# Loading a spectral filter in 18 loads of 2 pieces, each on half the partitions, in place of 28 loads of 3 pieces over all partitions

## Chip, cores and metric

The kernel runs on one core of a Trainium2 chip. The metric is the device time of one execution in microseconds (us), as the median of several runs. The spans and moments that profiles give are counted from the first instruction and come out about 1.8 us shorter than that time.

## The reference, cut to what matters

```python
x = A_x                                              # 1 x 2048 x 512, bfloat16
X = rfft2(layernorm(x)) * (w_r + 1j * w_i)           # the filter: 2048 x 257, real and imaginary part
h = x + irfft2(X)
h2 = h + MLP_over_the_rows(layernorm(layernorm(h)))  # two large products with B_w1, B_w2
```

Row 64q + r of the filter (q = 0 to 31) meets a spectrum row kept at free position r; row 64q + (64 − r) is its mirror. The kernel keeps 32 positions, and on each of the 128 partitions a fixed combination of q, of the half (itself or its mirror, `ss`), and of real or imaginary part (`reim`).

## The kernel before

The constants L and H of the transforms say which partition holds which combination:

```python
for jj, ss, sgn, j in kinds:
    ...
    for k2 in range(NS2):
        pre = 8 * k2 + 4 * jj + 2 * ss        # the partition; the imaginary part is at pre + 1
```

Neighbours in q are thus four partitions apart. The filter is loaded in three pieces of rows; each load fills 32 partitions, four apart, with runs of 512 bytes:

```python
pieces = [(0, 8), (8, 18), (18, 32)]
for pi, (ta, tb) in enumerate(pieces):
    for comp, wsrc in enumerate((A_w_r, A_w_i)):
        wv = wsrc.rearrange("(q r) k -> q r k", r=64)
        for reim in range(2):
            parts = [(0, ta, tb, wv[:, ta:tb, 1:257])]
            lo = ta
            if ta == 0:
                parts.append((1, 0, 1, wv[:, 32:33, 1:257]))
                lo = 1
            parts.append((1, lo, tb, wv[:, 64 - lo:64 - tb:-1, 1:257]))
            for ss, a, b, src in parts:
                dma(..., "sp", W[2 * ss + reim:NP:4, a:b, comp, :], src, ..., group=f"W{pi}", wgroup=f"W{pi}")
```

The loads of one piece share one semaphore, so a reader waits for the whole piece. The readers are 16 multiplications on VectorE, called P0 to P15 below:

```python
def emit_P(c):          # reads filter rows 2c and 2c + 1
    return eng.tensor_tensor(P[:, :, :, :], x.unsqueeze(2).broadcast_to(...), W[:, 2 * c:2 * c + 2, :, :], ALU.mult)
# VectorE's fixed order: ... P0 P1 ... P3 P2 ... P4 ... P5 ... P7 P6 ... P9 P8 ... P10 P11 ... P13 P12 ... P14 P15
```

PE turns each P into 8 short products (I0 to I15, in a fixed order too). Beside the filter, GpSimd's queue loads the biases of the MLP, that of the first product in single elements of 2 bytes, that of the second in runs of 32 bytes:

```python
gate = [o for o in K.ops if o.name == "Ye15"]        # a ScalarE copy near 16 us
dma("ld_b1a", "pool", B1s[:, 0:10], B_b1[0:1280].rearrange("(t p) -> p t", p=NP), 2560, ..., after=gate)
```

## Time and profile before

| | before |
|---|---|
| time, median | 130.94 us in the first 3 runs, 130.69 in the 6 around the comparison |
| span of the profiled run | 129.0 us |
| filter loads: number, last issued, last landed | 28, 25.95 us, 30.1 us |
| VectorE's wait for the filter | 1.75 us, at P9 |
| last product of the filter stage on PE | 37.68 us |
| granted clock | 1.0 |

In the profile, PE is the matmul engine, PEld its weight loads, DVE VectorE, ACT ScalarE, POOL GpSimd and SP or SPq the sync engine and its queue. A timeline row gives start, duration, what was done, how often, and in brackets the idle time just before with what ended it. A windows row gives a stretch and its length; the busy time of PE, PEld, DVE, ACT and POOL; then the granted clock, the share of the 16 DMA engines, and GB/s. The lines themselves are shown in the prediction.

### The profile page before, as it was taken

Reading aid. Unit: us, or ns where it says so; the run is one execution under the profiler, and the core shown is the slowest. Engines: PE = TensorE matmul, PEld = TensorE weight load, DVE = VectorE, ACT = ScalarE, POOL = GpSimd, SP = SyncE. Lnnn points to the kernel's source line nnn. Section 1 sums busy time; section 2 is a strip of 40 time slices with the busy share of each in tenths; the row PEclk is TensorE's granted clock in tenths of the full one; section 3 lists DMA queues with packets and bytes.
Section 4 is the critical chain, followed back from the end, with each engine's and each line's share of the span. In section 5 each row is a group of like instructions: output and inputs, shape, how many; then the busy total and the mean of one; then the engine's idle time right before and its main releaser. Section 6 shows DMA issues by size and latency. Waiting matters only on the chain.

```text
span 129.0 us, 2045 instructions
## 1 busy us (share of the span) xinstructions
PE 122.8 (95%) x786; PEld 74.6 (58%) x786; DVE 65.0 (50%) x141; ACT 65.0 (50%) x137; POOL 12.5 (10%) x33
## 2 busy tenths in 40 slices
PE   6998979999899999999999999999999999999990
PEld 2356657778576655555544444456666666666660
DVE  1689949986978999968650000000422423323322
ACT  4789879999868999897777712222000000000000
POOL 0068970220000000000000000000000000000000
PEclk9999999999999999999999999999999999999999
DMA  3999888899999999999100000000112111121121
GB/s 91 357 393 366 253 208 179 231 340 387 407 425 425 417 418 409 239 401 394 41 0 0 0 0 0 5 0 0 41 50 72 41 67 60 41 81 41 41 84 41
DMA packets 16505, 22.71 MB, mean 176 GB/s; under 512 B 1552, under 2 KB 12304, under 8 KB 16368
## 3 DMA queue, kind: packets, MB, share of 16 engines
q1 hardware_dynamic: 15808, 21.66, 48.2%
q10 hardware_dynamic: 576, 0.92, 2.1%
q0 software_dynamic: 112, 0.01, 0.4%
q8 instruction: 6, 0.10, 0.3%
q14 instruction: 3, 0.02, 0.1%
HBM read 20.49 MB, written 2.10 MB: 175 GB/s over the span
## 4 chain that ended last, share of the span: by engine, by line
PE 71%; SPq 18%; DVE 3%; DMA 3%; issue 2%; DVEq 0%
PE ps L844 29%; PE ps L962 28%; SPq L490 18%; PE ps L771 5%; DMA W<-in_A_w_i_dram 3%; PE ps L692 3%; PE ps L808 2%; DVE P L674 2%; PE ps L968 2%; PE ps L911 1%; DVE TT L709 1%; DVE OUT L974 1%; PE ps L864 0%; PE ps L533 0%; PE ps L801 0%
## 5 line engine op out<-in xcount | busy, mean ns | idle before, releaser
L844 PE MATMUL ps<-HH,W 128*128 128x512 bf16 (+1 forms) x170 | 39.6, 379 | 0.0
L962 PE MATMUL ps<-GT,W 128*128 128x512 bf16 (+1 forms) x165 | 35.9, 379 | 0.0
L974 DVE SCALAR_TENSOR_TENSOR OUT<-ps,B2f,H 128x512 bf16<-128x512 f32 x16 | 12.0, 752 | 46.7 <-PE ps L962 24.4
L962 PEld LDWEIGHTS ps<-GT,W 128*128 128x128 bf16 (+1 forms) x165 | 23.8, 144 | 11.9
L844 PEld LDWEIGHTS ps<-HH,W 128*128 128x128 bf16 (+1 forms) x170 | 16.9, 100 | 17.5 <-issue 0.2
L944 ACT ACTIVATE GT<-ps,B1f 128x512 bf16<-128x512 f32 (+1 forms) x11 | 7.0, 692 | 12.7 <-PE ps L844 12.7
L818 DVE TENSOR_TENSOR H<-ps,X 128x512 bf16<-128x512 f32 x14 | 9.7, 691 | 4.0 <-PE ps L808 3.4
L824 ACT ACTIVATE SQ<-H,nm 128x512 bf16<-128x512 bf16 x14 | 10.1, 720 | 2.7 <-DVE H L818 2.4
L674 DVE TENSOR_TENSOR P<-Xsb,W 128x1024 bf16<-128x1024 bf16 x16 | 10.4, 684 | 1.9 <-DMA W<-in_A_w_i_dram 1.8
L559 DVE BATCH_NORM_STATS2 st<-X 128x6 f32<-128x512 bf16 x13 | 8.3, 679 | 3.2 <-DMA X<-in_A_x_dram 3.2
L692 PE MATMUL ps<-Hm,P 128*128 128x128 bf16 x128 | 9.1, 220 | 0.7 <-DVE TT L709 0.6
L781 ACT ACTIVATE EO<-ps 128x512 bf16<-128x512 f32 x15 | 8.8, 586 | 0.9 <-PE ps L771 0.7
L637 PE MATMUL ps<-E,Y 128*128 128x256 bf16 x64 | 8.5, 273 | 0.7 <-ACT Y L607 0.7
L771 PE MATMUL ps<-GD,TT 128*128 128x256 bf16 x60 | 9.0, 273 | 0.0
L692 PEld LDWEIGHTS ps<-Hm,P 128*128 128x128 bf16 x128 | 7.4, 98 | 2.7 <-issue 1.1
L533 PE MATMUL ps<-WM 128*128 128x512 bf16 (+1 forms) x20 | 7.6, 540 | 1.2 <-DVE eps L525 1.2
L593 PE MATMUL ps<-FS,X 128*128 128x256 bf16 x64 | 7.8, 273 | 0.5 <-POOL FS L577 0.5
L665 ACT ACTIVATE Xsb<-ps 128x1024 bf16<-128x1024 f32 (+1 forms) x9 | 8.0, 886 | 0.7 <-PE ps L652 0.4
L577 POOL TENSOR_SCALAR FS<-F,rs 128x256 bf16<-128x256 bf16 x16 | 7.4, 481 | 7.5 <-DMA F<-c_F 6.9
L641 ACT ACTIVATE Bsb<-ps 128x512 bf16<-128x512 f32 x13 | 7.3, 594 | 1.2 <-PE ps L637 1.2
L771 PEld LDWEIGHTS ps<-GD,TT 128*128 128x128 bf16 x60 | 5.8, 98 | 3.0 <-ACT EO L781 0.2
L593 PEld LDWEIGHTS ps<-FS,X 128*128 128x128 bf16 x64 | 5.4, 97 | 3.0 <-POOL FS L577 1.5
(70 smaller groups left out, 98.3 us busy)
## 6 DMA issues: line engine op xcount, KB each, us to landing
W<-in_B_w_dram SPq DMA_DIRECT2D x8, 688.0 KB, 11.0
W<-in_B_w_dram SPq DMA_DIRECT2D x10, 512.0 KB, 17.7
out_dram<-OUT SPq DMA_DIRECT2D x16, 128.0 KB, 1.7
X<-in_A_x_dram SPq DMA_DIRECT2D x4, 256.0 KB, 6.2
F<-c_F SPq DMA_DIRECT2D x4, 256.0 KB, 6.6
IF<-c_IF SPq DMA_DIRECT2D x1, 1024.0 KB, 6.5
W<-in_A_w_r_dram SPq DMA_DIRECT2D x4, 224.0 KB, 4.2
W<-in_A_w_i_dram SPq DMA_DIRECT2D x4, 224.0 KB, 4.2
```

The lines of the kernel that those rows point to most:

```text
L490: return eng.dma_start(dst, src)
L593: r = eng.matmul(ps[:, b, 256 * u:256 * u + 256].rearrange("p (a b) -> p a b", a=2), X[:, n2, 128 * t:128 * t + 128], fr if t < 2 else fa, ...
L637: r = eng.matmul(o, Y[:, k, c, :], E[:, k, :].rearrange("p (h r) -> p h r", h=2), start=(i == 0), stop=(i == 3), skip_group_check=True)
L674: return eng.tensor_tensor(P[:, :, :, :], x.unsqueeze(2).broadcast_to([NP, 2, 2, 256]), W[:, 2 * c:2 * c + 2, :, :], ALU.mult)
L692: r = eng.matmul(o, P[:, h, m, par::2], Hm[:, v, m, :].rearrange("p (m r) -> p m r", r=4), start=(h == 0 and m == 0 and (par == 0 or b != ...
L771: r = eng.matmul(o, TT[:, q, n2, par, :], GD[:, par, q, :], start=(i == 0), stop=(i == 3), skip_group_check=True)
L781: return eng.activation(eo[:, :], ps[:, bE, :], ACT.Copy)
L818: K.op(f"h{n2}", "dve", lambda e, eng: eng.tensor_tensor(H[:, n2, :], ps[:, bA, :], X[:, n2, :], ALU.add), ins=[ps[:, bA, :], X[:, n2, :]] ...
L824: K.op(f"sq{n2}", "act", lambda e, eng: eng.activation(sq[:, :], hsrc, ACT.Square, bias=nm[:, n2, 0:1], accum_out=s2t[:, n2, 0:1]), ins=[h ...
L844: return eng.matmul(ps[0:Mt, bank, :], W1[:, n2, 128 * t:128 * t + Mt], HH[:, n2, :], start=(n2 == 0), stop=(n2 == 15), skip_group_check=True)
L962: r = eng.matmul(ps[:, b, :], W2[t][0:Kt, n2::16], GT[0:Kt, t, :], start=(t == 0), stop=(t == NFT - 1), skip_group_check=True)
L974: K.op(f"fin{n2}", "dve", lambda e, eng, n2=n2, b=b: eng.scalar_tensor_tensor(OUT[:, n2, :], ps[:, b, :], B2f[:, n2:n2 + 1], H[:, n2, :], ...
```

## The change

Its intent is fewer issues on the sync engine: the mirrored half moves to partitions 64 to 127. The odd mirrored row 32 is then one load for both `reim`, and the pieces become two.

```diff
-                pre = 8 * k2 + 4 * jj + 2 * ss
+                pre = 64 * ss + 4 * k2 + 2 * jj
 (the same once more, for H)
-    pieces = [(0, 8), (8, 18), (18, 32)]
+    pieces = [(0, 12), (12, 32)]
     for pi, (ta, tb) in enumerate(pieces):
         for comp, wsrc in enumerate((A_w_r, A_w_i)):
             wv = wsrc.rearrange("(q r) k -> q r k", r=64)
 (the loads of before, shown above, go)
+            lo = max(ta, 1)
+            for ss, src in ((0, wv[:, ta:tb, 1:257]), (1, wv[:, 64 - lo:64 - tb:-1, 1:257])):
+                a = lo if ss else ta
+                for reim in range(2):
+                    dma(f"ld_w{comp}_{pi}_{ss}_{reim}", "sp", W[64 * ss + reim:64 * ss + 64:2, a:tb, comp, :], src, ...)
+            if pi == 0:
+                dma(f"ld_w{comp}_{pi}_m", "sp", W[64:128, 0, comp, :], wv[:, 32, 1:257].unsqueeze(1).broadcast_to([32, 2, 256]), ...)
```

More of the change, by code (lines that the diff above doesn't have):

```diff
@@ L98, in build_consts @@
             for k2 in range(NS2):
-                pre = 8 * k2 + 4 * jj + 2 * ss
+                pre = 64 * ss + 4 * k2 + 2 * jj
                 if special:
@@ L513, in build_kernel @@
             wv = wsrc.rearrange("(q r) k -> q r k", r=64)
-            for reim in range(2):
-                parts = [(0, ta, tb, wv[:, ta:tb, 1:257])]
-                lo = ta
-                if ta == 0:
-                    parts.append((1, 0, 1, wv[:, 32:33, 1:257]))
-                    lo = 1
-                parts.append((1, lo, tb, wv[:, 64 - lo:64 - tb:-1, 1:257]))
-                for ss, a, b, src in parts:
-                    dma(f"ld_w{comp}_{pi}_{reim}_{ss}_{a}", "sp", W[2 * ss + reim:NP:4, a:b, comp, :], src, 32 * 512 * (b - a),
+            lo = max(ta, 1)
+            for ss, src in ((0, wv[:, ta:tb, 1:257]), (1, wv[:, 64 - lo:64 - tb:-1, 1:257])):
+                a = lo if ss else ta
+                for reim in range(2):
+                    dma(f"ld_w{comp}_{pi}_{ss}_{reim}", "sp", W[64 * ss + reim:64 * ss + 64:2, a:tb, comp, :], src, 32 * 512 * (tb - a),
                         prio=1.0 + pi, group=f"W{pi}", wgroup=f"W{pi}")
+            if pi == 0:
+                dma(f"ld_w{comp}_{pi}_m", "sp", W[64:128, 0, comp, :], wv[:, 32, 1:257].unsqueeze(1).broadcast_to([32, 2, 256]), 64 * 512,
+                    prio=1.0 + pi, group=f"W{pi}", wgroup=f"W{pi}")
     K.op("mk_eps", "dve", lambda e, eng: eng.memset(eps[:, 0:1], LN_EPS), outs=[eps[:, 0:1]], occ=70.0, lat=130.0, prio=0)
```

## The prediction

> **What bounds the kernel now.** I started with the page's busy shares: PE 122.8 of 129.0 us. The granted clock is 1.0 throughout. The kernel is one long row of PE work, so a change counts only where PE is held back by something else. The chain that ended last says where that is:
>
> ```profile
> PE 71%; SPq 18%; DVE 3%; DMA 3%; issue 2%; DVEq 0%
> ```
>
> From about 30 us on the chain is PE. Before that it is the issue of DMAs by the sync engine (SPq), closed by one transfer. The chain in order of time shows the joint:
>
> ```profile
> 25.29 0.63 SPq L490
> 25.95 4.18 DMA W<-in_A_w_i_dram
> 30.23 1.29 DVE P L674 x2
> 31.52 0.60 DVE TT L709
> ```
>
> So the last filter load is issued at 25.95, lands 4.18 us later, and two filter multiplications (P, L674) start at that instant. The list of waits gives the price, in us in total, times, longest:
>
> ```profile
> DVE P L674 <- DMA W<-in_A_w_i_dram: 1.8, 1, 1.8
> ```
>
> Only one multiplication waits for the filter. VectorE's timeline shows which, and what is behind it (start, duration):
>
> ```profile
> 19.86 1.29 DVE L674 TENSOR_TENSOR P<-Xsb,W 128x1024 bf16<-128x1024 bf16 x2
> ...
> 26.42 1.28 DVE L674 TENSOR_TENSOR P<-Xsb,W 128x1024 bf16<-128x1024 bf16 x2
> 27.78 0.69 DVE L709 CAST TT<-ps 128x512 bf16<-128x512 f32 x1
> 30.23 1.29 DVE L674 TENSOR_TENSOR P<-Xsb,W 128x1024 bf16<-128x1024 bf16 x2 [1.75 <-DMA W<-in_A_w_i_dram]
> 31.44 0.68 DVE L709 CAST TT<-ps 128x512 bf16<-128x512 f32 x1
> 32.04 1.28 DVE L674 TENSOR_TENSOR P<-Xsb,W 128x1024 bf16<-128x1024 bf16 x2
> ```
>
> P number c reads filter rows 2c and 2c+1, and VectorE's fixed order is P0 P1 P3 P2 P4 P5 P7 P6 P9 P8 and so on. The pair at 26.42 is P7, P6; the pair at 30.23 is P9, P8, and P9 is the first to need the third piece (rows 18 to 31). From 30.23 VectorE has no gap until 36.9, and PE idles 0.63 us for it. The stage therefore follows VectorE, and the end of the kernel follows the stage.
>
> The loads' issue, from the sync engine's timeline:
>
> ```profile
> 6.76 4.00 SPq L490 DMA_DIRECT2D W<-in_A_w_r_dram  x6
> 10.80 3.87 SPq L490 DMA_DIRECT2D W<-in_A_w_i_dram  x6
> 14.71 2.59 SPq L490 DMA_DIRECT2D W<-in_A_w_r_dram  x4
> 17.35 3.69 SPq L490 DMA_DIRECT2D W<-in_A_w_i_dram  x4
> 21.08 2.64 SPq L490 DMA_DIRECT2D W<-in_A_w_r_dram  x4
> 23.76 2.82 SPq L490 DMA_DIRECT2D W<-in_A_w_i_dram  x4
> ```
>
> 28 issues take 19.8 us, some 0.66 each (one of 1.70), whether 16 KB or 224 KB. Is it the issue or the transfer that limits? The windows (last two columns: share of the 16 DMA engines, GB/s) say: mostly the issue.
>
> ```profile
> 14.00:16.00 2.00, 2.00 (x19) 1.32 (x16) 1.78 (x3) 1.60 (x4) 1.84 (x6) 1.00 0.77 209
> 16.00:18.00 2.00, 1.31 (x13) 1.09 (x12) 0.57 (x1) 1.30 (x4) 1.76 (x6) 1.00 0.83 205
> 26.00:28.00 2.00, 2.00 (x26) 1.49 (x25) 1.92 (x4) 2.00 (x4) 0.78 (x2) 1.00 1.14 341
> ```
>
> While 128 to 160 KB pieces are issued, only 205 to 209 GB/s move; once 224 KB pieces come, the same kind of packet reaches 341. By the trace's transfer records the filter is 8192 packets of 512 B (4.19 MB), nearly all of 27 ns, up to 674 of them in a microsecond. They start at 12.3 us, behind x and the constants.
>
> **What the Trainium skill says.** (1) "SBUF — State Buffer", section "Door 1: The DMA port swizzle": 64 neighbouring partitions (0 to 63, or 64 to 127) reach only 8 of SBUF's 16 DMA ports; it measured 196 GB/s for partitions 0 to 63 against 328 for all, with 218 as the asymptote. Every filter load of before steps through the partitions by 4 over all 128, so over all 16 ports, and 341 GB/s agrees. No load of before lies in one half, so its trace can't confirm the 196. (2) The same page, "Can I just issue two DMAs to hit both halves?": two DMAs, one per half, gained 6% together, "they serialize". (3) "DMA: Bandwidth & Descriptors", "Queues, rings and completion order": a DMA is split over up to 16 engines and each takes its ring in order, so loads of one half queue ahead of loads of the other. The lines above show no contrary case. (4) Same page, "Rules for kernel authors": coalesce small transfers. The 16 KB issues, as dear as 224 KB ones, agree.
>
> **The change, part by part.**
> Removed: 10 issues, 10 × 0.66 = 6.6 us of the sync engine. 18 issues end at 6.76 + 18 × 0.66 = 18.6, instead of 26.6. From 12.3 us on about 8 loads are already queued, so the transfers, not the issues, set the pace: 300 GB/s of issue in the first piece (196 KB per 0.66 us), 500 in the second.
> Kept: 8192 packets, all instructions of the compute engines and their shapes (L and H only have rows permuted).
> Moved: first, the pieces are rows 0 to 11 (3072 packets) and 12 to 31 (5120). P7 and P6, at 26.42, now need the last load of all; before, they needed the second of three pieces. Second, each load lies in one half of the partitions, on 8 ports.
> What the ports make of it, an estimate: a port that passes 27.2 GB/s (the skill's figure) takes 512 / 27.2 = 18.8 ns per packet, and two engines share it, so 37.6 ns instead of 27 for each engine. 8 ports give 425 packets per us, 218 GB/s; the skill's own measurement, 196, gives 383. I take 405 (207 GB/s).
> First piece: 12.3 + 3072 / 405 = 19.9, plus about 0.6 until the last packet counts: 20.5, where P0 now starts at 19.86. A short wait.
> Second piece: 12.3 + 8192 / 405 + 0.6 = 33.1. P7 wants it at 26.42, so VectorE waits 6.7 us. Behind P7 the stage needs what it needs now without the 1.75 us wait: 37.68 (end of the stage's matmuls) − 26.42 − 1.75 = 9.5 us, all VectorE's. Little is made up in the wait, because PE's next products need P6. The stage ends at 33.1 + 9.5 = 42.6 instead of 37.7: +4.9.
> After the stage: the identity, GD, IF (1.3 MB) and W1 are issued earlier but are carried after the filter. At 420 GB/s the first three end some 3.2 us after 33, W1's first part 1.7 us later, about 38.5. They are needed from 42.6 on: no new wait. With the port limit, then, 130.9 + 4.9 = 135.8.
>
> **Rivals.**
> A: the ports don't bind, because engines drift apart or a port takes more. For it: 27 ns packets without any collision in before, though I don't know which engine serves which partition. Then 8192 packets at about 620 per us last 13.2 us, land at 12.3 + 13.2 + 0.6 = 26.1, just before P7 at 26.42. The 1.75 us are won, or 1.0 if small transfers interfere: 129.2 to 130. More than 1.75 can't be won, since VectorE has hardly a gap before and PE hardly one after. That is 1.3%, inside the 2%.
> B: the engines fall onto even fewer ports at a time (neighbouring rows of one load share a port in fours). Below 200 GB/s each 10 GB/s costs about one us: at 180 GB/s the load ends at 36.2 and the kernel takes 139. No line speaks for it, but the split of rows over engines isn't visible.
> C: it is hidden anyway, as most of DMA is: against it, P9 already waits now, and the change moves the dependency two steps forward, to P7.
>
> **Range and chances.** About 0.65 for the port limit (134.5 to 137.5), 0.27 for A (129 to 131) with partial limits up to 133 in between, 0.08 for B. A case with faster by over 2% needs 2.6 us, more than the visible wait. I predict 135.0, a little under the sum because a partial limit is likelier than B, and 129.0 to 138.5 as the range.
>
> **What would show it.** The last filter issue near 18.6 us. In the windows from 14 to 32 us a steady 195 to 220 GB/s although loads are queued (A: over 300). Packets of some 37 ns. A wait of VectorE's P for W of 5 to 8 us, once, at P7, ending near 33 (A: none or under 1). No gap longer than before at P9. The rest of the kernel moved bodily by about 5 us, with PE's busy time of L844 and L962 the same. The prediction is wrong if P7 starts on time, or if W1 or IF arrives late and takes the wait over.

## The result

The changed kernel takes 139.14 us (138.48 to 140.21, 6 runs) against 130.69 (130.22 to 132.38, 6 runs). The ratio is 1.0666, 95% interval 1.0612 to 1.072: slower by 6.7%. Ratios here are the mean time of one kernel's fast runs over that of the other's of the same rounds, so they are not quite the ratio of the medians quoted. The profiled run is a fast one, with a span of 137.1 us.

The chain that ended last, on the changed kernel's page, to be set against the same line of before:

```profile
PE 71%; SPq 18%; DMA 6%; DVE 1%; issue 1%; DVEq 0%
```

DMA's share has doubled. The same chain in order of time (start, duration) shows the joint:

```profile
26.53 7.96 DMA W<-in_A_w_i_dram
34.58 1.30 DVE P L673 x2
35.93 1.89 PE ps L691 x16
```

The last filter load takes 7.96 us to land instead of 4.18, and the multiplications behind it start at 34.58. The list of waits (total, times, longest):

```profile
DVE P L673 <- DMA W<-in_A_w_i_dram: 7.9, 2, 7.0
...
PE ps L691 <- DVE P L673: 6.5, 2, 5.7
```

Before, VectorE waited 1.8 us once, and PE had no wait for a P; the one that followed from it was 0.63 us, for a later copy of VectorE's. PE now stands still for 5.66 us, from 30.27 on:

```profile
35.93 1.89 PE L691 MATMUL ps<-Hm,P 128*128 128x128 bf16 x16 [5.66 <-DVE P L673]
```

VectorE's timeline says at which P, and what follows:

```profile
20.97 1.29 DVE L673 TENSOR_TENSOR P<-Xsb,W 128x1024 bf16<-128x1024 bf16 x2 [0.97 <-DMA W<-in_A_w_i_dram]
...
34.58 1.29 DVE L673 TENSOR_TENSOR P<-Xsb,W 128x1024 bf16<-128x1024 bf16 x2 [6.96 <-DMA W<-in_A_w_i_dram]
...
40.55 0.69 DVE L708 CAST TT<-ps 128x512 bf16<-128x512 f32 x1 [1.08 <-PE ps L691]
```

It is P7, with 6.96 us, and a short wait at P0. The third row is new: after P7, VectorE is held up by PE (1.08 us here, and 0.32 and 0.33 later), which in the same stage of before cost it 0.19 us at most. The sync engine's timeline:

```profile
6.76 4.90 SPq L490 DMA_DIRECT2D W<-in_A_w_r_dram  x5
11.71 4.41 SPq L490 DMA_DIRECT2D W<-in_A_w_i_dram  x5
16.15 4.28 SPq L490 DMA_DIRECT2D W<-in_A_w_r_dram  x4
20.48 7.37 SPq L490 DMA_DIRECT2D W<-in_A_w_i_dram  x4
```

18 issues take 21.1 us, more than the 28 of before: single ones take up to 2.78 us. So the issue seems to follow the transfer now. The windows:

```profile
14.00:16.00 2.00, 2.00 (x19) 1.42 (x18) 1.91 (x4) 1.74 (x4) 1.92 (x6) 1.00 1.24 229
...
22.00:24.00 2.00, 2.00 (x30) 1.45 (x28) 1.81 (x4) 1.09 (x4) 0.00 (x0) 1.00 1.27 111
...
36.00:38.00 2.00, 2.00 (x18) 1.91 (x19) 2.00 (x4) 1.08 (x2) 0.00 (x0) 0.50 1.00 414
```

Three things show here. The DMA engines are busy (share over 1.2) at 229 GB/s, where 341 was reached before. Between 22 and 24 us even that halves, to 111. And from 33.46 to 40.29 us the granted clock is 0.50; it falls 3.2 us after PE has stopped. Before it was 1.0 throughout.

In the span, 129.0 to 137.1, the 8.1 us divide like this: P7 at 34.58 instead of 26.42, less the 1.75 us wait at P9 that is gone, is 6.4. From P7 to the stage's last product it takes 10.8 us (34.58 to 45.40) instead of 9.5, which is 1.3. The rest of the kernel, 91.7 us against 91.3, is 0.4 longer. PE's part of it is the same (88.2 us in both); the difference lies behind PE's last product, 3.5 us against 3.1, and its cause is open.

### The profile page after: what moved, and what is told of

The parts are those of the page before. It is cut to its first block, busy times and chain, and to the rows that moved or that the text cites. A ratio compares the mean times of both kernels' runs of the same rounds, so it can differ in the third digit from the quotient of the medians.

```text
span 137.1 us, 2025 instructions
## 1 busy us (share of the span) xinstructions
PE 123.6 (90%) x777; PEld 75.7 (55%) x786; DVE 65.2 (48%) x141; ACT 65.5 (48%) x137; POOL 12.1 (9%) x33
## 4 chain that ended last, share of the span: by engine, by line
PE 71%; SPq 18%; DMA 6%; DVE 1%; issue 1%; DVEq 0%
PE ps L843 27%; PE ps L961 26%; SPq L490 18%; DMA W<-in_A_w_i_dram 6%; PE ps L770 5%; PE ps L691 5%; PE ps L807 2%; PE ps L967 2%; PE ps L651 1%; PE ps L910 1%; DVE P L673 1%; PE ps L636 1%; DVE OUT L973 1%; PE ps L863 0%; PE ps L800 0%
## 5 line engine op out<-in xcount | busy, mean ns | idle before, releaser
L691 PE MATMUL ps<-Hm,P 128*128 128x128 bf16 x128 | 9.9, 236 | 6.5 <-DVE P L673 6.5
L943 ACT ACTIVATE GT<-ps,B1f 128x512 bf16<-128x512 f32 (+1 forms) x11 | 7.0, 692 | 12.7 <-PE ps L843 11.8
L691 PEld LDWEIGHTS ps<-Hm,P 128*128 128x128 bf16 x128 | 8.4, 106 | 8.4 <-DVE P L673 6.6
L636 PE MATMUL ps<-E,Y 128*128 128x256 bf16 x64 | 9.0, 282 | 0.7 <-ACT Y L606 0.7
L532 PE MATMUL ps<-WM 128*128 128x512 bf16 (+1 forms) x19 | 7.0, 521 | 1.2 <-DVE eps L524 1.2
```

The source lines that it names most:

```text
L636: r = eng.matmul(o, Y[:, k, c, :], E[:, k, :].rearrange("p (h r) -> p h r", h=2), start=(i == 0), stop=(i == 3), skip_group_check=True)
L691: r = eng.matmul(o, P[:, h, m, par::2], Hm[:, v, m, :].rearrange("p (m r) -> p m r", r=4), start=(h == 0 and m == 0 and (par == 0 or b != ...
```

## The experiments

My theory after the result had three parts: (a) a load that lies in one half of the partitions is slow because two DMA engines share each of its 8 ports (the trace doesn't name engines or ports, so the runs can show that the limit belongs to one half, not how the engines are spread); (b) the small bias loads cause the dip at 22 to 26 us; (c) the lowered clock stretches the stage. Rivals: the larger pieces or the fuller queue are slow by themselves; the dip is the filter's own; the stage is VectorE's, whatever the clock.

One measure comes from the trace's records of single transfers: the filter is 8192 packets of 512 bytes in all kernels. How many started in a given microsecond:

| kernel | 14 | 18 | 22 | 23 | 26 | last load landed, us |
|---|---|---|---|---|---|---|
| before | 528 | 388 | 444 | 471 | 672 | 30.1 |
| changed | 468 | 418 | 199 | 223 | 432 | 34.5 |
| e1 stride 4, two pieces | 669 | 512 | 522 | 607 | 532 | 28.6 |
| e2 halves, three pieces | 481 | 491 | 367 | 447 | 439 | 34.9 |
| e3 halves, bias loads late | 463 | 416 | 469 | 412 | 410 | 32.9 |
| e6 quarters | 481 | 394 | 179 | 198 | 354 | 36.1 |
| e10 halves from two queues | 470 | 429 | 608 | 673 | 667 | 32.3 |

### e1 and e2: the layout and the pieces apart

e1 is the kernel before with two pieces (and so 20 loads):

```diff
-    pieces = [(0, 8), (8, 18), (18, 32)]
+    pieces = [(0, 12), (12, 32)]
```

> The kernel before with the changed kernel's two pieces (rows 0 to 11 and 12 to 31), each load still stepping by 4 partitions over all 128: 20 loads. Theory 1 (the loads of one half of the partitions are slow by their ports): packets stay at 27 ns, over 550 per us, the last filter load lands near 26 to 27 us, P7 waits under 1 us, kernel 129.3 to 130.6 us. Theory 2 (the fuller queue or the larger pieces are slow, or putting P7 behind the last load costs by itself): P7 waits 3 us or more, kernel 134 or more.

e2 is the changed kernel with the opposite edit (26 loads).

> The changed kernel with the three pieces of before (8, 10 and 14 rows), each load in one half: 26 loads. Theory 1 (ports): about 400 to 430 packets per us, the filter is complete near 34 us, the wait moves from P7 to P9 (wanted at 28.5) and is 5 to 6 us, kernel 134.5 to 137 us. Theory 2 (pieces): under 132 us.

e1: 131.18 us, ratio 1.006 (1.003 to 1.009), clock 1.0. P7 on VectorE's timeline:

```profile
28.66 1.29 DVE L674 TENSOR_TENSOR P<-Xsb,W 128x1024 bf16<-128x1024 bf16 x2 [2.54 <-DMA W<-in_A_w_i_dram]
```

e2: 135.63 us, ratio of the fast runs 1.0301 (1.0252 to 1.0349). Two of its four runs count as slow, that is over 1.5% above its fastest (136.8 and 137.7, at a clock of 0.975, against 134.2 and 134.5), the profiled one among them. The clock of that run fell only at 37.38 us, after the last filter load had landed (34.9), so I read the packets and the waits before that from it:

```profile
26.18 0.69 DVE L673 TENSOR_TENSOR P<-Xsb,W 128x1024 bf16<-128x1024 bf16 x1 [2.08 <-DMA W<-in_A_w_i_dram]
...
35.01 1.30 DVE L673 TENSOR_TENSOR P<-Xsb,W 128x1024 bf16<-128x1024 bf16 x2 [4.54 <-DMA W<-in_A_w_i_dram]
```

The same two pieces cost 0.6% with loads over all partitions and 6.7% with loads in halves; three pieces in halves cost 3.0%. (The 3.0% is from the two runs at a clock of 0.99 to 1.0, whereas all six of the changed kernel had the lowered clock; the median of all four runs of e2 is 135.63 us.) The layout is what slows the transfer: the last load lands at 28.6 in e1 and at 34.9 in e2. The pieces decide where the wait falls (P7, or P4 and P9). But e1 misses my numbers as well: I expected the last load at 26 to 27 us and a gain, and it landed at 28.6, with P7 waiting 2.54 us. So even with all ports this choice of pieces has nothing to give.

### e3: the bias loads late

```diff
-    dma("ld_b1a", "pool", ..., after=gate)
+    late = [o for o in K.ops if o.name == "Ie15_1"]     # the end of the filter stage
+    dma("ld_b1a", "pool", ..., after=late)              # likewise ld_b1b and ld_b2
```

> The changed kernel with the three small loads of the biases (2-byte elements) sent after the filter stage instead of beside the filter. If they cause the dip of the filter's transfer between 22 and 26 us (down to 111 GB/s, some 650 packets short of the steady rate, worth 1.5 us), the dip vanishes, P7 starts near 33.1 and the kernel takes 137.0 to 138.0 us. If the dip has another cause, P7 stays at 34.6 and the time at 139.1.

137.82 us (136.5 to 138.29), ratio 1.0548 (1.0466 to 1.063). The windows:

```profile
22.00:24.00 2.00, 2.00 (x28) 1.49 (x26) 1.84 (x4) 1.59 (x3) 0.00 (x0) 1.00 1.25 226
24.00:26.00 2.00, 2.00 (x29) 1.49 (x27) 2.00 (x4) 1.72 (x4) 0.00 (x0) 1.00 1.24 222
...
36.00:38.00 2.00, 2.00 (x15) 0.96 (x13) 1.94 (x4) 1.19 (x2) 0.00 (x0) 0.50 1.02 417
```

The dip is gone (226 GB/s where 111 were), P7 starts at 33.04 instead of 34.58, so (b) holds: three loads of 7 KB in all cost 1.5 us here. The clock still falls to 0.50, from 32.67 to 39.50.

### e4 and e5: PE kept busy in the wait

e4 gives PE 18 throw-away matmuls of 512 columns ahead of I6, e5 does that on top of e3:

```diff
 def emit_I(c):
     P = Pb[c % NB]
+    if c == 6:
+        emit_warm("x", 18, bank_I(6, 0), 20, strict=True)
-  ... C10p I6 I5 ...
+  ... C10p wmx I6 I5 ...
```

> The changed kernel with 18 throw-away matmuls of 512 columns (some 3.9 us) where PE waits for P6. If the granted clock of 0.5 from 33.4 to 40.3 us, after that wait, costs 1.3 us of the filter stage, the clock stays at 1.0, P7 still starts near 34.6, the stage from there to its last product takes 9.5 us instead of 10.8, kernel 137.6 to 138.2. If the stage is VectorE's whatever PE's clock: 139.1.

> Both e3's and e4's edits in the changed kernel: bias loads late and 18 throw-away matmuls while PE waits. If the ports' rate alone makes the 4.9 us of the prediction, and the small loads and the lowered clock make the rest, then P7 starts near 33.0, the clock stays at 1.0 since the gap left for PE is under 1 us, the stage's last product ends near 42.5 and the kernel takes 135.3 to 136.3 us. If the clock drops all the same or costs nothing: 137 to 138 us, as with e3.

e4: 138.66 us, ratio 1.0645 (1.0595 to 1.0695). It tells little: the fill ended at 33.7 but P6 only at 36.1, and the clock still fell in the profiled run, from 35.96 to 39.37. Two of the four runs kept it at 1.0 (138.40 and 138.62; the others 138.70 and 139.56), which is too small a difference to judge; at a clock of 1.0 I had expected 137.6 to 138.2. I had made the fill too short.

e5: 136.07 us (135.62 to 136.85), ratio 1.042 (1.0365 to 1.0474), clock 1.0. The same window as e3's last row:

```profile
36.00:38.00 2.00, 2.00 (x32) 1.72 (x32) 2.00 (x4) 2.00 (x4) 0.00 (x0) 1.00 1.02 417
```

P7 starts at 33.19, as in e3 (33.04), yet the last product ends at 42.44 instead of 44.23: 9.25 us from P7 against 11.2. PE does 32 matmuls in the two microseconds where e3 does 15. So (c) holds, the clock alone is worth 1.7 us between e3 and e5 in the median, and the rival (the stage is VectorE's at any clock) falls.

### e6: 32 neighbouring partitions

Each load on 32 neighbouring partitions (20 loads), L and H to match:

```diff
-    pre = 64 * ss + 4 * k2 + 2 * jj            # imaginary part at pre + 1
+    pre = 64 * ss + 2 * k2 + jj                # imaginary part at pre + 32
-    W[64 * ss + reim:64 * ss + 64:2, ...]
+    W[64 * ss + 32 * reim:64 * ss + 32 * reim + 32, ...]
```

> The changed kernel with each load on 32 neighbouring partitions (0 to 31, 32 to 63 and so on) instead of every second one of 64; 20 loads. If it is the ports as the skill maps them, 32 neighbours reach the same 8 ports as 64: some 420 to 440 packets per us where nothing disturbs, 138 to 140 us. If the step between partitions or the spread over them decides, the rate differs by more than 15%: nearer 600 or nearer 220.

139.63 us, ratio 1.067 (1.0624 to 1.0716), the same as the changed kernel. Outside the dip the packets run at the same rate, 390 to 490 per us. A quarter of the partitions is no slower than a half, and the step between partitions (1 or 2) doesn't matter, which fits the port map that the prediction quotes. The dip of the bias loads is longer (98 GB/s from 22 to 24 us and 137 from 24 to 26); why, no run shows.

### e10: both halves in flight from two queues

e3 with the four mirrored loads of the second piece issued by ScalarE:

```diff
-    dma(f"ld_w{comp}_{pi}_{ss}_{reim}", "sp", ...)
+    dma(f"ld_w{comp}_{pi}_{ss}_{reim}", "act" if pi and ss else "sp", ...)
-  ScalarE: ... Ye12 Ye15 Be0 ...
+  ScalarE: ... Ye12 Ye15 ld_w0_1_1_0 ld_w0_1_1_1 ld_w1_1_1_0 ld_w1_1_1_1 Be0 ...
```

> e3 (halves, bias loads late) with the four mirrored loads of the second piece issued by ScalarE after Y is evacuated (near 17 us, 1.8 us of ScalarE's time), so that loads of both halves are in flight at once from two queues. If two engines sharing one port is what costs, mixing the halves frees the other 8 ports: over 520 packets per us from about 19 us on, filter complete before 30, P7 under 30.5, kernel 132 to 134.5. If loads of one half are slow for another reason, or the halves serialize as the skill says: 450 per us at most, P7 at 32 or later, 136.5 to 139.

The times scatter, 132.71 to 145.77 (median 135.18), and three of four count as slow, so there is no ratio. A window of the profiled run:

```profile
24.00:26.00 2.00, 2.00 (x20) 1.13 (x19) 0.82 (x2) 1.47 (x3) 0.00 (x0) 0.67 1.15 346
```

From 22 to 27 us the packets run at 608 to 680 per us, from 23 us on all of 27 ns, and a transfer that was stuck at 207 to 226 GB/s in e3 moves at 328 to 361, though every load still lies in one half. In these microseconds the two queues start packets in nearly equal numbers (337 and 336 from 23 to 24 us). This is the most direct evidence for (a): with loads of both halves moving side by side, the limit goes. It doesn't go at once: from 20 to 22 us both queues already had packets in flight (95 and 369 in the first microsecond, 190 and 225 in the second), and the rate was still 464 and 415. So a second queue by itself isn't enough; what set the rate free at 22 us is open. It is also one profiled run, and two queues with loads of the same half weren't tried. As a kernel it is no use: the four issues held ScalarE for 4.6 us (I had said 1.8), PE stood still meanwhile, the clock fell, and the last load landed only at 32.3 and P7 started at 32.37 (I had said under 30.5). From 28 us on just 3 to 27 filter packets per us are left beside the large packets of the next loads; that the alternation between the two queues starves them is my reading, not shown.

### e7, e8, e9, e11: looking for the gain

e7 is e1 with the bias loads late, e8 the kernel before with the bias loads late. e9 and e11 cut the filter into 16 and 16 rows (stride 4), with and without late bias loads.

> e1 (all 16 ports, two pieces) with the bias loads late. In e1 the filter took until 29.3 us and P7 waited 2.5 us, though the ports were free. If the small loads hold it up: filter complete near 27 us, P7's wait under 1 us, kernel 129.0 to 130.0. If the packets' own rate (about 500 per us over the whole) is the limit: 131, as e1.

> The kernel before with the bias loads late and nothing else. If they also slow the filter there (one issue of 1.70 us at 18.0, 158 GB/s between 20 and 22 us), the last filter load lands 1 us or more earlier, P9's wait of 1.75 us falls under 1, kernel 129.0 to 130.0 against 130.4. If the issue alone sets the pace: unchanged.

> The kernel before with two pieces of 16 rows (steps of 4 partitions, all 16 ports, 20 loads) and the bias loads late. In e1 and e7 the filter was complete at 28.3 to 28.6 us, about when P9 is wanted (28.5), and with 16 rows in the first piece P9 is the first to need the second. First piece: 4096 packets at about 550 per us from 11.8, so near 19.8, when P0 is wanted. Both waits under 0.4 us, the 1.75 us of before gained: 128.6 to 129.4 us. If something else takes the wait's place: 130 or more.

> The same with the bias loads left where they were. If the small loads only matter when the ports are short, it is as fast as the one with late bias loads, within 0.4 us: 128.6 to 129.8.

| run | us, median | ratio (95%) | last load landed | wait of P for the filter in the profiled run |
|---|---|---|---|---|
| e7 | 130.33 | 0.9969 (0.9933 to 1.0005) | 28.3 | 1.81 at P7 |
| e8 | 130.37 | 0.998 (0.9946 to 1.0015) | 29.6 | 1.27 at P9 |
| e9 | 130.53 | 0.9991 (0.9946 to 1.0036) | 26.4 | none |
| e11 | 130.73 | 0.9956 (0.9913 to 0.9999) | 28.5 | 2.25 at P0 (a slow run) |

In e7 the profile names ScalarE as the releaser of P7; as P7 starts 0.1 us after the last load lands, I read it as the load. None has its median in the range that I expected. Over all ports the small loads cost little: between e1 and e7 P7 moves by 0.25 us, and between the kernel before and e8 P9 by 0.5 us, not by the 1.5 of e3. e9 does remove the wait, and its profiled run has 129.38 us, but the others go up to 131.18, and no profile shows what they wait for. e11's slow run shows one way to lose it: with 16 rows in the first piece P0 waited 2.25 us, PE paused, and the clock was at 0.5 from 23.24 to 26.65. PE's pause was only 2.08 us long:

```profile
22.53 1.41 PE L692 MATMUL ps<-Hm,P 128*128 128x128 bf16 x16 [2.08 <-DVE P L674]
```

### e12: the version that the runs point to

Three pieces and stride 4 as before, cut so that each piece is wanted later, and the bias loads late:

```diff
-    pieces = [(0, 8), (8, 18), (18, 32)]
+    pieces = [(0, 10), (10, 20), (20, 32)]
```

> The kernel before with its three pieces cut at rows 10 and 20 instead of 8 and 18 (28 loads, steps of 4 partitions) and the bias loads late. In e8 the last load landed at 29.6 us; cut at 20, the first multiplication to need it is P10, wanted at 30.4 in before without the wait, and P5 instead of P4 is the first to need the second piece. No wait of P for W over 0.3 us, the 1.75 us of before gained: 128.6 to 129.4 us, faster by 1.0 to 1.4%. If it stays at 130.2 or more, the wait was not worth its length.

129.67 us (129.48 to 130.01), ratio 0.9951 (0.9917 to 0.9986). The row of P10, the first to need the third piece:

```profile
30.23 1.28 DVE L674 TENSOR_TENSOR P<-Xsb,W 128x1024 bf16<-128x1024 bf16 x2
```

It has no wait. The stage's last product ends at 36.45, 1.2 us before that of before, and the span is 127.8 against 129.0. It is the fastest kernel, but by half a per cent, not by the 1.0 to 1.4 that I expected: 1.2 us of the 1.75 come out in the profiled runs, and 0.6 us in the mean of the timed ones. The profile shows why not all: with the wait gone, PE never rests from 24 us to the end of the stage, the pairs of P follow each other every 1.97 us instead of 1.80, and from P7 to the last product it takes 10.2 us (26.28 to 36.45). Part of the wait had lain behind PE's own work. It is within the 2% that count as the same.

## Why the prediction was wrong

The direction and the main mechanism held; the size did not, 139.14 against 135.0 and a range that ended at 138.5.

**What held.** The port step did. In e3, which has no disturbance, the 8192 packets took from 11.8 to 31.9 us, 408 per us, against my 405; the asymptote of 218 GB/s that the prediction quotes corresponds to 425. P7 was the one to wait, as said, and in e3 it starts at 33.04 where I had 33.1. That it is so close is partly luck: I had the first packet at 12.3 us (on the trace's own zero it is 11.8) and 0.6 us from the last packet to P7 (it is 1.1), and the two errors cancel. W1 and IF took no wait over. With both disturbances removed, e5 measures 136.07 where the working gave 135.8.

**What failed, first: the second piece's term.** "12.3 + 8192 / 405 + 0.6 = 33.1" took the port rate as undisturbed for 20 us. The small loads were in the profile before, and I put them down to rival A alone ("1.0 if small transfers interfere"). In the changed kernel they cost 1.5 us: 34.58 against 33.04 in e3.

**Second: what comes behind P7.** "Behind P7 the stage needs what it needs now without the 1.75 us wait: … 9.5 us, all VectorE's" carried a duration over from a trace in which PE rested for 0.63 us at most in this stage. A VectorE wait of 7 us leaves PE idle for 5.66, the clock is halved for 6.8 us from 3.2 us into that pause, and PE becomes the slower of the two: 10.8 us instead of 9.5. e5 shows 9.25 once PE is kept busy. Its worth is 1.3 us in the profile of the changed kernel and 1.7 in the medians of e3 and e5. And 9.5 us was no fixed need of the stage either: without any wait (e12) it takes 10.2 us, all PE's.

So 4.9 + 1.5 + 1.3 us, and 0.4 in the rest of the kernel that stays open, make the 8.1 of the span. The two failed steps weigh about the same. "Little is made up in the wait" was thus too mild: something is lost.

**Wrong without consequence.** "18 issues end at … 18.6": the last issue was at 26.53. Where the filter's transfer ended later, so did the issue: at 22.5 us in e9 (20 loads over all ports), 26.3 in e3 and 27.9 in the changed kernel (18 in halves). "Packets of some 37 ns": their median was 45 ns, against 27 before, but the records overlap (a share of the DMA engines of 1.25), so rate and length don't follow from each other. "About 38.5" for W1 should be 37.9 by its own terms (33 + 3.2 + 1.7). And rival A was too hopeful: with all 16 ports the filter landed at 28.6 (e1), not at 26.1, so its 129.2 to 130 would not have come true.

## To carry to other kernels

Before counting DMA issues saved, look at which partitions each single load covers: a load that stays in one half of the partitions ran at some 410 packets per us here, where up to 676 were seen with loads over all partitions (e9), and up to 680 where a second queue moved the other half at the same time (e10). When a change makes one engine wait for several microseconds, don't carry over the durations behind the wait; ask whether PE idles in it, for then the clock may fall and the work after it is slower: here, from 6 us on, it fell in each of the seven profiled runs with a pause of PE of 2.08 us (e11) or more, and after no pause of 1.72 us (e12) or less. The limit is not sharp: with e4's fill, whose pause was 2.42 us in the profiled run, two of the four runs kept the clock. And the wait here was removed without a shorter transfer, by cutting the pieces so that each is wanted after it lands (e12), though that was worth only half a per cent.

## What the Trainium skill lacked or had wrong

- "SBUF — State Buffer", "Can I just issue two DMAs to hit both halves?": it says that two DMAs, one in each half, gain 6% and serialize, from several issuing engines too. In e10's one profiled run, with loads of the two halves in flight from two queues, the packets of 512 bytes ran at up to 680 per us (346 GB/s), against 387 to 473 per us with one queue and nothing else in the way (e3). It did so only from 22 us on; in the 2 us before, with packets of both queues in flight too, and with one queue, the statement held. The port table itself ("Door 1: The DMA port swizzle") was right for both halves and quarters: 408 packets per us, 209 GB/s.
- "TensorE: Matmul & The Clock Gate", "Part 1: The HAM clock gate": it has the clock fall after an idle window of some 3.4 us. In e4 PE had stopped at 33.7 and the clock fell at 35.96, so the 3.4 us before it were about one third busy (with throw-away matmuls on zeros). In e11 it fell at 23.24 after a pause of 2.08 us, with real products before it. The longest pause of PE that the clock outlived in a profiled run was 1.72 us (e12). The halved stretches lasted 6.83 us (changed kernel, e3) or 3.41 us (e4, e11), two and one of the page's windows.
- "DMA: Bandwidth & Descriptors": I found nothing in it on the issuing engine being held back when loads from HBM are behind. Issues that take 0.6 us took up to 2.78 us here, and 18 of them took longer than 28 had.
- The same page says ("Rules for kernel authors") that a strided last dimension makes one descriptor per element, not what they cost others: three bias loads of 7 KB in all cost the filter 1.5 us when it lay in halves (e3), and 0.25 to 0.5 us when spread over all ports (e1 against e7, before against e8). Why it differs is open.
